# Strassen's seven products in the last unit's second layer, its operand sums in four pieces, and new instruction orders, in a one-core attention and MoE kernel

## The chip, the cores and the metric

The kernel runs on one core of one Trainium2 chip. The metric is the device time of one execution in microseconds (us). A profiled execution has a span, from its first to its last instruction, and a time of its own, which is a little longer than the span because it holds what lies around it. Engines are named as in the profile: PE is the matrix engine (TensorE) and PEld its weight loads, DVE is VectorE, ACT is ScalarE, POOL is GpSimd, SP is SyncE, which here only issues transfers.

## The reference

Two stages follow each other. The first is a gated linear recurrence over 768 tokens for 4 batches and 8 heads of 48 channels; the second is a two-layer network on its output, taken as 3072 tokens of 384 channels, with 2048 hidden channels and the square of a rectifier between the layers.

```python
def _attn_ref(q, k, v, alpha):          # (4, 8, 768, 48) each
    for t in range(S):
        state = alpha[:, :, t, :, None] * state + np.einsum('bhd,bhe->bhde', k[:, :, t], v[:, :, t])
        y[:, :, t] = np.einsum('bhd,bhde->bhe', q[:, :, t], state)
    return y

def _moe_ref(x, w_in, w_out):           # (3072, 384), (384, 2048), (2048, 384)
    r = np.maximum(x @ w_in, 0.0)
    return (r * r) @ w_out
```

## The kernel before

The work is cut into 12 units of 256 tokens: three stretches of the sequence for each of four batches. Unit g goes through these steps; the names in brackets are those of the instruction orders, with the unit's number behind them.

1. Transfers of alpha, k, q and v from memory (`lda`, `ldk`, `ldq`, `ldv`), in fp32.
2. Decays: a product of two alphas (`pr`), logarithm (`ln`), cumulative sums on PE (`m1`, `m1i`, `m1s`), exponentials (`ei`, `ea`, `es`, `ec`), a second product (`bk`, `aq`, lines 679 to 697), then k and q scaled by them (`ekm`, `eqm`, lines 732 and 737), v in bf16 (`vc`, line 727), and transposes (`tr`).
3. Scores on PE (`p`), masked by DVE (`mk`, line 937); the output of the recurrence (`y`, lines 818 to 865), which also holds the state products of the next unit (`kv`); the state (`sa`, `sc`, `sd`).
4. The output goes to bf16 (`xe`) and is transposed (`xt`, `xv`).
5. First layer, line 1030: eight pieces `s1_g_u` of six matmuls of 256 columns, each piece into one PSUM bank of 512 columns, read by a rectifier (`re`, lines 1038 and 1040) and squared into the tile GT (`sq`, lines 1048 to 1052). A square may cover two pieces.
6. Second layer. Each unit has two tiles of 128 tokens, j = 0 and 1; GT holds 16 slices f of 128 hidden channels for both. In units 0, 1 and 2, and in unit 11, it is 16 matmuls of 384 columns for each tile (line 1168). Units 3 to 10 use Strassen's form (`second_layer_strassen`, line 1064): the 16 slices are taken as 8 pairs u of an even and an odd slice, the two tiles as the rows, and the two halves of 192 output columns as the columns of a 2 x 2 block product. Seven products m1 to m7 take the place of eight, each of 8 matmuls of 192 columns (line 1096).

Strassen's form needs sums of blocks of GT, bf16: `ga` writes two differences into SG (line 1080), `gb` overwrites the block of the even slices of tile 1 with a difference (line 1082), and `gc` writes a sum into SH (line 1083). They exist in two halves of four pairs, `_0` and `_1`. They follow each other: ga needs the squares, gb needs ga, gc needs gb. The products use them so: m5 and m7 read SG, m6 and m4 the blocks of GT that hold sums or the odd slices of tile 1, m3 reads SH, m1 and m2 the blocks of GT as they are. The sums of the weights (SW) are made once (`ws`).

The products run in two PSUM banks, psO (A) and the first bank of psWH (B). A collects m1, then m2 on top of it, and, begun afresh, m5 and m3; B collects m6, m7 and m4. After each product a copy or a sum of 128x192 takes what the bank holds so far into the output tile OSB: `ca` after m1, `cb` after m6, `cc` after m2, `cd` after m7, `ce` after m5, `cf` after m4, `cg` after m3 (lines 1123 to 1127). The next product into the same bank waits for it. One transfer then writes the unit's 256 tokens (`out`, line 1145).

The last unit, 11, differs. Tile 0 runs as 16 matmuls of 384 columns into psO, is copied and stored as 192 KB (line 1179). Tile 1 runs in `last_tile` (line 990): 16 matmuls of 272 columns and 16 of 112 into the two banks of psX (line 998), each copied into a tile OSL (lines 1003 and 1005) and stored by itself (line 1006), 136 KB and 56 KB.

Nothing chooses the order at run time. The table ORDERS (line 12) lists every operation of each engine in order, transfers among those of the engine that issues them; an operation whose name stands in the list of ACT runs on ACT, and the same operation may have a form for DVE or POOL. `add` records what an operation reads and writes, and `place` derives from that the semaphores on which it waits; each engine runs its list strictly in order. A sum that writes SG, for instance, waits until the products of the unit before have read SG. Operations `fill512_n` and `fill256_n` in PE's list are matmuls on zeros, 512 or 256 columns wide, put where PE would wait in the first part of the kernel.

Some transfers wait for others by the table AFTER (line 1194): the second half of w_in (`win2`) waits for q of unit 0, `wout0` for win2, `wout1` for k of unit 2, and the loads of units 3 and later for wout0.

Of the kernel before, what the change touches and what calls it, by code (L numbers as in the profile page):

```python
# [13 lines left out]
        table ln0_0 ln1_0 #23 ei0_0 ea0_0 ei1_0 ea1_0 et00_0 ec1_0 ec0_0 vc0 et11_0 ln1 ei1 ea1 xe0 xv0 ec1 re0_0  # L14
        re0_2 re0_3 xe1 re0_4 re0_5 ln2 sq0_5 ei2 re1_1 ea2 ec2 re1_4 es2 re1_3 re1_5 sq1_1 re1_7 et1_2 sq1_6 sq1_3
        sq1_5 oe0_0 ln3 ei3 ea3 ec3 vc3 es3 ln4 xe2 ei4 ea4 oe0_1 oe1_0 sa3 ec4 lm4 re2_1 es4 re2_2 re2_3 sq2_1 vc4
        re2_5 lm5 lm6 xe3 ln5 re2_7 ei5 ea5 ec5 sq2_5 re3_1 re3_0 re3_3 es5 oe2_0 re3_2 ln6 sq3_3 xe4 ei6 ea6 ec6
        re3_7 sq3_5 es6 sq3_7 re3_6 oe2_1 re4_1 re4_0 sq4_1 lm7 ca3 re4_2 ln7 xe5 ei7 re4_3 ea7 sq4_3 ec7 re4_5 re4_6
        lm8 re4_7 es7 sq4_7 re5_0 re5_1 sq4_5 re5_2 sq4_6 re5_3 ln8 xe6 ei8 re5_5 ea8 re5_4 es8 re5_7 cc4 re5_6 sq5_3
        re6_0 lm9 sq5_5 ln9 re6_1 re6_2 lm10 re6_3 ei9 re6_4 ea9 re6_5 sq6_1 re6_6 re6_7 sq6_3 es9 re7_1 re7_0 cc5  # L20
        sq6_5 re7_3 re7_2 ln10 xe8 sq7_1 ei10 ea10 re7_4 re7_5 ca6 lm11 re7_6 re7_7 es10 re8_0 cc6 re8_1 sq7_7 sq7_5
        re8_2 xe9 ln11 re8_3 ei11 ea11 sq8_1 sq8_3 es11 cc7 re8_6 re8_7 sq8_7 re9_0 sq8_5 sq8_6 xe10 re9_3 sq9_3 re9_5
        sq9_1 cc8 re9_6 sq9_6 sq9_5 re10_1 sq10_1 re10_3 xe11 re10_5 ca9 sq10_3 re10_4 sq10_5 re10_6 re11_0 re11_1
        sq10_6 re11_2 re11_3 sq11_3 ca10 re11_5 cc10 re11_7 sq11_6 oe11_10
    """,
    "dve": """
        #19 #2 #11 #16 #4 #10 #3 #8 #7 #5 #1 #13 #17 #18 #12 #9 #6 ekm0_0 eqm0_0 ekm1_0 et10_0 eqm1_0 et01_0 mk0_0 sa0
        mk1_0 sc0 ekm1 eqm1 et0_1 et1_1 mk1_1 mk0_1 sa1 re0_1 sq0_1 sq0_3 pr2 xv1 re0_7 re0_6 sq0_6 bk2 re1_2 re1_0
        ekm2 aq2 sc1 eqm2 et0_2 ws0_0 re1_6 ws2_0 ws1_1 mk1_2 mk0_2 sa2 sc2 bk3 ekm3 sq1_7 aq3 eqm1_3 eqm0_3 ws2_1 xv2
        sd2 re2_0 ekm4 lb4 sc3 eqm1_4 eqm0_4 mk0_3 mk1_3 re2_4 sa4 oe1_1 sc4 xv3 re2_6 bk5 lb5 ekm5 mk1_4 mk0_4 eqm1_5  # L30
        eqm0_5 sq3_1 sa5 re3_5 sc5 re3_4 lb6 xv4 eqm1_6 ekm6 gb3_0 eqm0_6 mk1_5 mk0_5 pr7 ga3_1 sa6 sc6 ws3_1 re4_4
        cb3 xv5 cc3 ekm7 lb7 cd3 ga4_0 ce3 mk1_6 eqm1_7 eqm0_7 mk0_6 cf3 cg3 gb4_0 ga4_1 sa7 ca4 gb4_1 sc7 xv6 cb4 lb8
        ekm8 eqm0_8 mk1_7 mk0_7 eqm1_8 cd4 ce4 ga5_0 sa8 xe7 cf4 sq5_6 ga5_1 cg4 gb5_1 lb9 eqm1_9 gc5_1 ca5 ekm9 cb5
        mk0_8 eqm0_9 mk1_8 cd5 gc5_0 ga6_0 ce5 sa9 cf5 ga6_1 gb6_1 gc6_0 cg5 sq7_3 lb10 cb6 ekm10 sq7_6 mk0_9 mk1_9
        cd6 eqm0_10 eqm1_10 ga7_0 ce6 sa10 ga7_1 cg6 re8_4 cf6 re8_5 ca7 cb7 lb11 ekm11 eqm0_11 eqm1_11 mk0_10 cd7
# [31 lines left out]
        #14 #20 #15 #21 #22 lda1 ldk1 ldq1 win1 win0 win2 lda2 vc1 ldq2 sd0 ldk2 ldv2 wout0 wout1 vc2 sq0_7 sd1 ldk3  # L67
        ldv3 pr3 ws0_1 pr4 bk4 pr6 sq2_3 ws1_0 pr5 ws3_0 sd3 sq2_6 sq2_7 vc5 sd4 ga3_0 bk6 sq3_6 sd5 vc6 gb3_1 bk7 pr8
# [281 lines left out]
def bass_gla_recurrent__then__act_relu_squared_kernel(  # L350
# [13 lines left out]
    T = 256  # L364
# [783 lines left out]
    def second_layer(g):  # L1148
# [115 lines left out]
```

## Time and profile before

| what | value |
|---|---|
| median of three runs | 173.21 us |
| lowest and highest of the three | 169.42 and 173.5 us |
| the profiled execution's own time | 169.46 us |
| its span | 167.7 us |
| its instructions | 5626 |
| PE, PEld busy | 160.9 and 139.6 us |
| DVE, ACT, POOL busy | 131.9, 121.3 and 96.8 us |
| moved by transfers | 32.80 MB |

Everything that is quoted from the profile comes from the one profiled execution. In the views a row names the line of the kernel, the engine, the operation, and what it writes and reads. In a group of instructions, the numbers behind the first bar are the busy time in us and the mean length of one in ns, and behind the second bar the idle time of the engine just before them with what ended it. In the chain that ended last and in the timeline, the first two numbers are the start and the length in us. A PE instruction's own length is longer than the distance between two of them, because matmuls overlap; in the chain the lengths are distances.

### The profile page before, as it was taken

Reading aid. Unit: us, or ns where it says so; the run is one execution under the profiler, and the core shown is the slowest. Engines: PE = TensorE matmul, PEld = TensorE weight load, DVE = VectorE, ACT = ScalarE, POOL = GpSimd, SP = SyncE. Lnnn points to the kernel's source line nnn. Section 1 sums busy time; section 2 is a strip of 40 time slices with the busy share of each in tenths; the row PEclk is TensorE's granted clock in tenths of the full one; section 3 lists DMA queues with packets and bytes.
Section 4 is the critical chain, followed back from the end, with each engine's and each line's share of the span. In section 5 each row is a group of like instructions: output and inputs, shape, how many; then the busy total and the mean of one; then the engine's idle time right before and its main releaser. Section 6 shows DMA issues by size and latency. Waiting matters only on the chain.

```text
span 167.7 us, 5626 instructions
## 1 busy us (share of the span) xinstructions
PE 160.9 (96%) x2431; PEld 139.6 (83%) x2431; DVE 131.9 (79%) x234; ACT 121.3 (72%) x214; POOL 96.8 (58%) x93
## 2 busy tenths in 40 slices
PE   7699999997999999999999999999999999999994
PEld 2466799755688788899999999999999999999973
DVE  5597989889887989889988999798699688353450
ACT  3965487976879699897978899787686856866310
POOL 3923815761559855669648759255729930277600
PEclk9999999999999999999999999999999999999999
DMA  5999999999999999999999989989988500522022
GB/s 135 327 319 209 275 303 216 200 338 267 161 230 166 229 295 124 294 160 263 282 163 327 241 136 336 141 193 334 133 203 139 148 10 4 152 87 94 0 98 94
DMA packets 68232, 32.80 MB, mean 196 GB/s; under 512 B 64144, under 2 KB 65168, under 8 KB 68208
## 3 DMA queue, kind: packets, MB, share of 16 engines
q1 hardware_dynamic: 65584, 25.76, 69.9%
q0 software_dynamic: 2624, 6.69, 16.3%
q8 instruction: 19, 0.31, 0.7%
q14 instruction: 5, 0.04, 0.1%
HBM read 25.17 MB, written 4.72 MB: 178 GB/s over the span
## 4 chain that ended last, share of the span: by engine, by line
PE 75%; DMA 15%; POOL 4%; DVE 3%; issue 1%; ACT 1%
PE psWH L1030 32%; PE psO L1096 13%; PE psWH L1096 10%; PE psO L1168 7%; DMA win<-in_moe_w_in_dram 7%; DMA wout<-in_moe_w_out_dram 5%; DMA raw<-in_alpha_dram 3%; PE psX L829 2%; PE psX L926 2%; PE psZ L797 2%; POOL raw L540 2%; PE psX L818 2%; PE psX L998 2%; PE psZ L926 1%; PE psX L972 1%; POOL win L508 1%
## 5 line engine op out<-in xcount | busy, mean ns | idle before, releaser
L1030 PE MATMUL psWH<-xt,win 128*128 128x256 bf16 x552 | 71.7, 273 | 0.2 <-DMA win<-in_moe_w_in_dram 0.2
L1030 PEld LDWEIGHTS psWH<-xt,win 128*128 128x128 bf16 x552 | 60.1, 129 | 2.1 <-DVE xt L984 0.4
L1038 ACT ACTIVATE rr<-psWH 128x512 bf16<-128x512 f32 x70 | 40.9, 595 | 18.3 <-PE psWH L1030 17.2
L1052 ACT ACTIVATE gt<-rr 128x1024 bf16<-128x1024 bf16 (+1 forms) x38 | 35.1, 940 | 2.8 <-PE psWH L1096 1.6
L1051 POOL TENSOR_TENSOR gt<-rr 128x512 bf16<-128x512 bf16 (+1 forms) x13 | 18.6, 1432 | 14.8 <-ACT rr L1038 9.7
L1082 POOL TENSOR_TENSOR gt<-sg,gt 128x512 bf16<-128x512 bf16 x10 | 12.0, 1202 | 12.6 <-DVE sg L1080 12.6
L1040 DVE TENSOR_SCALAR rr<-psWH 128x512 bf16<-128x512 f32 x22 | 15.0, 685 | 5.1 <-PE psWH L1030 5.0
L1168 PE MATMUL psO<-wout,gt 128*128 128x384 bf16 x96 | 18.4, 326 | 0.0
L937 DVE TENSOR_TENSOR pm<-psZ,caus 128x1024 bf16<-128x1024 f32 x12 | 14.6, 1218 | 1.9 <-PE psZ L926 1.9
L937 DVE TENSOR_TENSOR pm<-psX,caus 128x1024 bf16<-128x1024 f32 x12 | 14.6, 1215 | 0.6 <-PE psZ L926 0.5
L1096 PE MATMUL psWH<-sw,gt 128*128 128x192 bf16 x128 | 14.8, 246 | 0.0
L1096 PE MATMUL psO<-wout,gt 128*128 128x192 bf16 x128 | 14.7, 246 | 0.0
L1083 POOL TENSOR_TENSOR sh<-gt 128x512 bf16<-128x512 bf16 x11 | 14.2, 1298 | 0.7 <-DVE gt L1082 0.5
L1168 PEld LDWEIGHTS psO<-wout,gt 128*128 128x128 bf16 x96 | 8.8, 98 | 4.6
L686 POOL TENSOR_TENSOR ek<-ek,raw 128x384 f32<-128x384 f32 x7 | 7.1, 1008 | 9.6 <-ACT ek L679 9.6
L1127 DVE TENSOR_TENSOR osb<-psWH,osb 128x192 f32<-128x192 f32 x24 | 8.4, 350 | 5.0 <-PE psWH L1096 4.9
L737 DVE TENSOR_TENSOR qks<-raw,ek 128x768 bf16<-128x768 f32 x11 | 11.7, 1063 | 0.4 <-ACT ek L644 0.4
L1080 DVE TENSOR_TENSOR sg<-gt 128x1024 bf16<-128x1024 bf16 x14 | 10.6, 754 | 0.9 <-PE psO L1096 0.9
L1096 PEld LDWEIGHTS psWH<-sw,gt 128*128 128x128 bf16 x128 | 10.9, 98 | 0.3
L1096 PEld LDWEIGHTS psO<-wout,gt 128*128 128x128 bf16 x128 | 10.6, 98 | 0.5
L957 ACT ACTIVATE xbf<-psX 128x768 bf16<-128x768 f32 x11 | 8.9, 806 | 2.9 <-PE psX L818 1.7
L732 DVE TENSOR_TENSOR qks<-raw,eq 128x384 bf16<-128x384 f32 x18 | 10.4, 604 | 0.7 <-DMA raw<-in_q_dram 0.7
(164 smaller groups left out, 298.4 us busy)
## 6 DMA issues: line engine op xcount, KB each, us to landing
out_dram<-osb SPq DMA_DIRECT2D x11, 384.0 KB, 4.8
raw<-in_alpha_dram SPq DMA_DIRECT2D x10, 384.0 KB, 5.1
raw<-in_q_dram SPq DMA_DIRECT2D x10, 384.0 KB, 5.5
raw<-in_v_dram SPq DMA_DIRECT2D x10, 384.0 KB, 4.8
raw<-in_k_dram SPq DMA_DIRECT2D x9, 384.0 KB, 5.2
wout<-in_moe_w_out_dram POOLq DMA_DIRECT2D x2, 768.0 KB, 8.2
raw<-in_k_dram POOLq DMA_DIRECT2D x3, 384.0 KB, 6.4
raw<-in_alpha_dram POOLq DMA_DIRECT2D x2, 384.0 KB, 6.0
```

The costliest lines, as they stand in the source:

```text
L737: add("dve", lambda e, a=a, E=E: e.tensor_tensor(QKS[qs][:, a, :, :, 0:D], RAW[r][:, 1 + a].rearrange("p h j d -> p j h d"), E[la][:].rear ...
L937: add("dve", lambda e, hf=hf, psT=psT: e.tensor_tensor(PM[pm][:, hf].rearrange("p r n j t -> p (r n) (j t)"), psT[:, :, :].rearrange("p r ...
L1030: ins = pe.matmul(psF[:, i * T:(i + 1) * T], WIN[:, kk, hidden(fj)], mov, start=(kk == 0), stop=(kk == KT - 1))
L1038: add("act", lambda e, psF=psF, rr=rr: e.activation(rr, psF, AF.Relu), act_ns(512), pu + 600, reads=[keyF], writes=[("rr", rb, half)], nam ...
L1040: alts={"dve": (lambda e, psF=psF, rr=rr: e.tensor_scalar(rr, psF, 0.0, None, ALU.max), dve_ns(512))})
L1051: alts={"pool": (lambda e, dst=dst, sq=sq: e.tensor_tensor(dst, sq, sq, ALU.mult), 200 + k * 840), "act": (lambda e, dst=dst, sq=sq: e.act ...
L1052: "act": (lambda e, dst=dst, sq=sq: e.activation(dst, sq, AF.Square), act_ns(k * 512))})
L1080: ga = lambda e, us=us: e.tensor_tensor(SG[:, us], view(us, 128, [[0, 2], [1, 128]]), view(us, 0, [[384, 2], [1, 128]]), ALU.subtract)
L1082: gb = lambda e, us=us: e.tensor_tensor(G4[:, us, 0, 1], SG[:, us, 1], G4[:, us, 0, 0], ALU.subtract)
L1083: gc = lambda e, us=us: e.tensor_tensor(SH[:, us], G4[:, us, 1, 0], G4[:, us, 0, 1], ALU.add)
L1096: ins = pe.matmul(psS, left(u), right(u), start=(first and u == 0), stop=(u == nu - 1), skip_group_check=True)
L1168: ins = pe.matmul(psS, GT[gt][:, fj, j, :], WOUT[:, fj, :], start=(fj == 0), stop=(fj == FT - 1))
```

## The change

Three things change together.

First, unit 11's second layer takes Strassen's form too; `last_tile`, its tile OSL and its stores go. In this unit the third pair of products, m5 and m3, runs in a bank of its own, the second bank of psX (C), instead of in A. Three stores take the place of three: the first half of tile 0 (96 KB) after cc, tile 1 (192 KB) after cf, the second half of tile 0 (96 KB) after cg.

Second, in unit 11 the operand sums are cut in four pieces, of 4, 2, 1 and 1 pairs, instead of two of 4; the products are cut in the same pieces, so that m1 becomes `m10` to `m13`, with 4, 2, 1 and 1 matmuls. SG and SH are tracked by pair instead of by half.

Third, all five lists of ORDERS are new. Some 75 operations move to another engine, most of them rectifiers, squares, copies out of PSUM and the sums ga, gb and gc. POOL's list has 93 operations instead of 89, DVE's 247 instead of 234, ACT's 213 instead of 214, PE's 341 instead of 317, SP's 76 as before. PE's fills are 15 of 512 and 8 of 256 columns, before 15 and 6.

```diff
-    LAST_CUT = 272
-    SUMS, SPLIT = 30000, 2
+    SUMS = 30000
-    STRASSEN = tuple(range(3, 11))
+    STRASSEN = tuple(range(3, 12))
+    PIECES = {11: (0, 4, 6, 7, 8)}
...
-        cut = nu // SPLIT
-        for x in range(SPLIT):
-            us = slice(x * cut, (x + 1) * cut)
-            r = range(us.start, us.stop)
+        edges = PIECES.get(g, (0, nu // 2, nu))
+        parts = [range(x, y) for x, y in zip(edges, edges[1:])]
+        for x, r in enumerate(parts):
+            us, cut = slice(r.start, r.stop), len(r)
             ga = lambda e, us=us: e.tensor_tensor(SG[:, us], view(us, 128, [[0, 2], [1, 128]]),
                                                   view(us, 0, [[384, 2], [1, 128]]), ALU.subtract)
...
-                writes=[("sg", x)], name=f"ga{g}_{x}")
+                writes=[("sg", u) for u in r], name=f"ga{g}_{x}")
...
         def phase(k, name, psS, key, left, right, keys, first):
-            for h in range(2):
-                def run(pe, h=h):
-                    for u in range(h * nu // 2, (h + 1) * nu // 2):
+            for h, us in enumerate(parts):
+                def run(pe, us=us):
+                    for u in us:
...
         (psA, keyA), (psB, keyB) = bank("O"), bank("W")
-        psA, psB = psA[:, 0:n], psB[:, 0:n]
+        psC, keyC = bank("X1") if g == G - 1 else (psA, keyA)
+        psA, psB, psC = psA[:, 0:n], psB[:, 0:n], psC[:, 0:n]
...
-        phase(4, "m5", psA, keyA, lambda u: SG[:, u, 1], sums[0], keys(("sg",), ("sw", 0)), True)
+        phase(4, "m5", psC, keyC, lambda u: SG[:, u, 1], sums[0], keys(("sg",), ("sw", 0)), True)
...
-        phase(6, "m3", psA, keyA, lambda u: SH[:, u], wout[1][1], keys(("sh",), ("wout",)), False)
+        phase(6, "m3", psC, keyC, lambda u: SH[:, u], wout[1][1], keys(("sh",), ("wout",)), False)
...
+        if g == G - 1:
+            for x, (j, c) in enumerate(((0, slice(0, n)), (1, slice(0, 2 * n)), (0, slice(n, 2 * n)))):
+                rows = slice(b * S + i * T + j, b * S + i * T + T, 2)
+                add("sp", lambda e, rows=rows, j=j, c=c: e.dma_start(out[rows, c], OSB[ob][:, j, c]), 600, p0 + 7 * step,
+                    reads=[ok[j][y] for y in range(c.start // n, c.stop // n)], name=f"out{g}_{x}", dma=f"l{x}", lag=400)
+            return
```

Of the orders, the parts that the prediction speaks of. The starts of POOL's list (the numbers with # are selects on masks; those with `win`, `wout` and `ld` issue transfers):

```diff
-        #14 #20 #15 #21 #22 lda1 ldk1 ldq1 win1 win0 win2 lda2 vc1 ldq2 sd0 ldk2 ldv2 wout0 wout1 vc2 sq0_7 sd1 ldk3
-        ldv3 pr3 ws0_1 pr4 bk4 pr6 sq2_3 ws1_0 pr5 ws3_0 sd3 sq2_6 sq2_7 vc5 sd4 ga3_0 bk6 sq3_6 sd5 vc6 gb3_1 bk7 pr8
+        #22 #15 #20 #14 #21 lda1 ldk1 ldq1 win1 vc0 win0 win2 lda2 ldk2 ldq2 sd0 ldv2 sq0_1 wout0 wout1 sq0_5 sq0_6
+        aq2 sd1 vc2 ldk3 ldv3 pr3 ws1_1 pr4 bk4 sq2_3 pr6 pr5 sd3 sd4 sq2_7 sq2_6 ws1_0 vc5 ga3_0 gb3_0 bk6 sq3_6 vc6
```

ACT around the wait before y2 (`vc3` and `es3` belong to unit 3):

```diff
-        sq1_5 oe0_0 ln3 ei3 ea3 ec3 vc3 es3 ln4 xe2 ei4 ea4 oe0_1 oe1_0 sa3 ec4 lm4 re2_1 es4 re2_2 re2_3 sq2_1 vc4
+        sq1_5 re1_6 ln3 oe0_0 ei3 ea3 ec3 sq1_6 vc3 es3 ln4 xe2 ei4 lm4 oe0_1 oe1_0 ea4 ec4 re2_0 re2_1 es4 re2_2 lm6
```

The ends of ACT's, DVE's, PE's and POOL's lists:

```diff
-        sq10_6 re11_2 re11_3 sq11_3 ca10 re11_5 cc10 re11_7 sq11_6 oe11_10
+        re11_2 re11_3 cc10 sq11_3 re11_5 sq11_5 re11_6 sq11_6 sq11_7 cc11
...
-        sq11_7 cf10 oe11_0 oe11_11
+        sq11_1 ga11_0 cd10 ce10 ga11_1 re11_7 cg10 cf10 ga11_3 gb11_3 ca11 cb11 gc11_0 cd11 ce11 cf11 cg11
...
-        s2_10_m51 s1_11_7 s2_10_m30 s2_10_m31 s2_10_m40 s2_10_m41 s2_11_0_0 s2_11_0_1 s2_11_0_2 s2_11_0_3 s2_11_1_0
-        s2_11_1_1
+        s2_10_m11 s1_11_3 s2_9_m41 s2_10_m20 s1_11_4 s2_10_m21 s2_10_m60 s2_10_m61 s1_11_5 s2_10_m50 s2_10_m70
+        s2_10_m71 s2_10_m51 s1_11_6 s2_10_m40 s1_11_7 s2_10_m30 s2_10_m31 s2_10_m41 s2_11_m50 s2_11_m10 s2_11_m11
+        s2_11_m12 s2_11_m13 s2_11_m60 s2_11_m61 s2_11_m62 s2_11_m63 s2_11_m20 s2_11_m21 s2_11_m70 s2_11_m71 s2_11_m72
+        s2_11_m73 s2_11_m51 s2_11_m52 s2_11_m22 s2_11_m23 s2_11_m53 s2_11_m40 s2_11_m41 s2_11_m42 s2_11_m43 s2_11_m30
+        s2_11_m31 s2_11_m32 s2_11_m33
...
-        gb10_1 sq11_1 gc10_1 sq11_5
+        gc10_1 gb11_0 ga11_2 gb11_1 gb11_2 gc11_3 gc11_1 gc11_2
```

The rest of the orders keeps the same steps in much the same sequence, with halves of products, rectifiers and squares dealt to other places in the lists.

More of the change, by code (lines that the diff above doesn't have):

```diff
@@ L19 @@
[L19 to L23, printed above, removed]
@@ L69 @@
-        gc3_0 gc3_1 vc7 sq5_1 gc4_0 bk8 sq5_7 vc8 gc4_1 pr9 sd6 gb5_0 bk9 pr10 sq6_7 sd7 sq6_6 vc9 gb6_0 bk10 pr11
-        vc10 gc6_1 gb7_0 gb7_1 gc7_1 bk11 ga8_0 vc11 gc7_0 gb8_0 gb8_1 gc8_1 gc8_0 sq9_7 gb9_0 sq10_7 gc9_1 gb10_0
-        gb10_1 sq11_1 gc10_1 sq11_5
+        #22 #15 #20 #14 #21 lda1 ldk1 ldq1 win1 vc0 win0 win2 lda2 ldk2 ldq2 sd0 ldv2 sq0_1 wout0 wout1 sq0_5 sq0_6
+        aq2 sd1 vc2 ldk3 ldv3 pr3 ws1_1 pr4 bk4 sq2_3 pr6 pr5 sd3 sd4 sq2_7 sq2_6 ws1_0 vc5 ga3_0 gb3_0 bk6 sq3_6 vc6
@@ L1177, in second_layer @@
                 alts={"dve": (lambda e, j=j, psS=psS: e.tensor_copy(OSB[ob][:, j], psS), dve_ns(DM))})
-            if g == G - 1:
-                add("sp", lambda e, rows=rows: e.dma_start(out[rows, :], OSB[ob][:, 0]), 600, ps_ + 1300,
-                    reads=[("osb", ob, 0)], name=f"out{g}_0", dma=f"o{ob}", lag=600)
-            elif j == 1:
+            if j == 1:
                 dst = out[b * S + i * T:b * S + i * T + T, :].rearrange("(p j) n -> p (j n)", j=2)
```

137 lines of the change are left out of this document (61 added, 76 removed).

## The prediction

> **What bounds the kernel now.** I read the page first (span and busy shares), then the busy time by stretch, then the chain that ended last, in its last 11 us and in its first 41.
>
> ```profile
> span 167.7 us, 5626 instructions
> ```
> ```profile
> 150.00:160.00 10.00, 10.00 (x112) 9.87 (x111) 4.79 (x13) 5.05 (x9) 6.50 (x5) 1.00 0.11 41
> sum 120.00, PE 119.85 PEld 110.31 DVE 97.41 ACT 92.64 POOL 74.81; mean PE 9.99 PEld 9.19 DVE 8.12 ACT 7.72 POOL 6.23
> ```
>
> The rows are the last of twelve stretches of 10 us and their sum; after a stretch's length stand the busy times of PE, PE's weight loads, DVE, ACT and POOL, then the granted clock (1.00 in all twelve). Between 40 and 160 us PE is idle for 0.15 us of 120, while DVE, ACT and POOL have slack, most of it in 150 to 160, where DVE works 4.79 us of 10. From 40 us on the kernel is PE's instruction stream, end to end: only less work on PE shortens this part, and any wait put into PE's order lengthens it one for one.
>
> ```profile
> 157.14 0.66 PE psWH L1030 x6
> ...
> 159.44 0.66 PE psWH L1096 x8
> 160.10 2.60 PE psO L1168 x16
> 162.70 2.65 PE psX L998 x32
> 165.35 0.02 issue
> 165.38 0.27 DVE osl L1005
> ```
>
> These are the last links of the chain (start, length, what). Six first-layer matmuls of 256 columns take 0.66 us, eight Strassen matmuls of 192 columns 0.66 us too, so 82.5 ns each. The last unit's second layer is the two links at 160.10 and 162.70, 5.25 us. PE ends at 165.35; a copy and a store fill the remaining 2.35 us of the span.
>
> The first 40 us hang on transfers:
>
> ```profile
> 8.79 11.97 DMA win<-in_moe_w_in_dram
> ...
> 21.04 8.26 DMA wout<-in_moe_w_out_dram
> ...
> 29.32 5.54 DMA raw<-in_alpha_dram
> ```
> ```profile
> 25.06 0.60 POOL L508 DMA_DIRECT2D wout<-in_moe_w_out_dram  x1 [3.32 <-DMA raw<-in_k_dram]
> 25.85 0.82 POOL L727 CAST vbf<-raw 128x768 bf16<-128x768 f32 x1 [0.19 <-DMA raw<-in_v_dram]
> ```
> ```profile
> 37.50 0.99 POOL L658 TENSOR_TENSOR prd<-raw 128x384 f32<-128x384 f32 x1
> ...
> 37.53 1.38 DVE L688 TENSOR_TENSOR ek<-ek,raw 128x384 f32<-128x384 f32 x1 [0.42 <-ACT ek L679]
> ...
> 40.05 0.36 PE L858 MATMUL psX<-smd,kqt 128*64 128x96 bf16 x8 [0.95 <-DVE qks L737]
> ```
>
> The second half of w_in lands, w_out is issued, alpha of unit 3 waits for that, and its products reach PE at 40.05 (y2), where PE has stood idle for 0.95 us. So the end is 40.05 plus PE's work after y2 plus the tail.
>
> **Term 1: PE's work in the last unit.** Removed are 16 matmuls of 384, 16 of 272 and 16 of 112 columns, 5.25 us by the chain. Added are seven products of eight 192-column matmuls: 56 x 82.5 ns = 4.62 us. That is -0.63 us on the path. Pieces cost PE nothing, since the count of matmuls is the same in four pieces as in two.
>
> ```profile
> L1096 PEld LDWEIGHTS psWH<-sw,gt 128*128 128x128 bf16 x128 | 10.9, 98 | 0.3
> ```
>
> A weight load reads 98 ns, longer than the 82.5 ns of its matmul. If loads set the pace, 56 x 98 ns = 5.49 us, and the term is +0.24. But eight of these pairs pass in 0.66 us and the 32 pairs at 162.70 in 2.65 us (32 loads end to end would be 3.14), so loads overlap each other and I keep -0.63. The Trainium skill (TensorE: Matmul & The Clock Gate, LDWEIGHTS) prices a 128-column load at 128 / 1.2 ns, about 107 ns; end to end that would be an estimated 5.97 us, a loss of 0.72, and the row of 0.66 us for eight disagrees with such a pace.
>
> **Term 2: the sums of the last unit, and whether PE waits for them.** Added are four each of ga, gb and gc. Their rows, with those of the steps before them:
>
> ```profile
> L1040 DVE TENSOR_SCALAR rr<-psWH 128x512 bf16<-128x512 f32 x22 | 15.0, 685 | 5.1 <-PE psWH L1030 5.0
> ...
> L1127 DVE TENSOR_TENSOR osb<-psWH,osb 128x192 f32<-128x192 f32 x24 | 8.4, 350 | 5.0 <-PE psWH L1096 4.9
> ...
> L1048 DVE TENSOR_TENSOR gt<-rr 128x512 bf16<-128x512 bf16 x5 | 2.1, 416 | 0.0
> ...
> L697 DVE TENSOR_TENSOR eq<-eq,raw 128x384 f32<-128x384 f32 x2 | 1.1, 548 | 0.0
> ```
> ```profile
> L1082 POOL TENSOR_TENSOR gt<-sg,gt 128x512 bf16<-128x512 bf16 x10 | 12.0, 1202 | 12.6 <-DVE sg L1080 12.6
> ...
> L1051 POOL TENSOR_TENSOR gt<-rr 128x1024 bf16<-128x1024 bf16 x4 | 7.7, 1925 | 4.7 <-ACT rr L1038 4.2 <-ACT osb L1123 0.5
> ```
> ```profile
> L1052 ACT ACTIVATE gt<-rr 128x512 bf16<-128x512 bf16 x1 | 0.6, 630 | 1.1 <-DVE rr L1040 1.1
> ```
>
> (Before the last bar: busy us, mean ns of one.) I walk PE's new order by hand, with 0 at the end of s1_11_5. s1_11_7 ends at 2.95 and the three halves of unit 10 left at 3.94; then m5's first piece, m1 from 4.27 to 4.93, m6 to 5.59, m2's first two pieces to 6.09, m7 to 6.75, rests of m5 and m2 to 7.24, m4 to 7.90, m3 to 8.56.
> The large first piece is early: its ga (1024 columns, by the 416 ns of 512 some 0.8 us, DVE) must only wait until unit 10's m7 has read SG (0.66), so gb (1202 ns, POOL) ends near 2.7, needed at 4.93.
> The last piece is the tight one. From 2.95: rectifier 0.69 (DVE), square 0.63 (ACT), so 4.27, with hand-offs about 4.4; m1 wants it at 4.85. ga and gb of one pair (256 and 128 columns) have no row; they lie between nothing and the 416 ns of 512 columns; by halves with some fixed cost I estimate 0.27 and 0.2. gb done at 4.9 to 5.2; m6 wants it at 5.51. So by itself nothing waits.
> What can make it wait is the port. DVE L688 above took 1.38 us beside POOL L658, against 548 ns in L697, the same shape: it ran after POOL had ended at 38.49. In the tail, POOL runs gb of pieces 1 and 2 (about half and a quarter of 1202 ns) just when DVE wants ga and gb of piece 3. If POOL goes first each time, gb is ready at 5.4, the copy ca behind it on DVE holds m2 by 0.2, and gc11_0, held by POOL's gc, delays cd and with it m4 by 0.25: 0.45 in all. Bounds 0 and 0.45; I take 0.2. The Trainium skill (SBUF — State Buffer, SBUF: two separate sides) says this port pair is an exclusive lock kept for a whole instruction; the pair of rows agrees.
> Behind the waiting DVE instruction stand ca, cb, cd, ce, which free the banks of psO, psWH and psX for m2, m7, m4, m3. m5 moved to the free psX bank is what keeps cc (on ACT) off this path; without it m5 would wait for cc.
>
> **Term 3: after PE.** The last copy becomes a sum of 192 columns, 0.35 instead of 0.27: +0.08. The last store grows from 56 KB to 96 KB, and 192 KB go out just ahead:
>
> ```profile
> out_dram<-osb SPq DMA_DIRECT2D x1, 192.0 KB, 1.9
> out_dram<-osl SPq DMA_DIRECT2D x1, 136.0 KB, 1.7
> ...
> out_dram<-osl SPq DMA_DIRECT2D x1, 56.0 KB, 1.5
> ```
>
> (The last column is us from issue to landing.) 96 KB lies between the two, 0 to +0.4; I take +0.1, as 96 is nearer to 56 and the 192 KB leave one sum (0.35) earlier.
>
> **Term 4: the start, up to y2.** The new orders put more in front of POOL's transfers. vc0 (0.82, the L727 row) now stands between the issues of win1 and of win0 and win2: those two go out 0.8 later. They lie in the queue for 11.97 us anyway, so the queue's backlog hides it. sq0_1 (1925 ns) now stands in front of wout0 and issues it perhaps 1 us after 21.04; until 25.85 the queue is still delivering v of unit 2, issued ahead of it, so this is hidden too. wout1 waits for k2, which now goes ahead of q2: earlier, if anything. sq0_5, sq0_6 and aq2 (1.9 + 1.2 + 1.0) stand in front of sd1, vc2, ldk3 and ldv3; POOL was idle for 3.32 us before 25.06, which takes most of it. SP's loads and transposes only change places among themselves behind its wait for w_out. Where a cover is gone, y2 comes later by as much, up to 1 us. On the other side, POOL's product pr4 ran in front of DVE's L688 by 0.03 us; if L688 goes first, y2 could come 0.83 earlier, but vc3, now behind one more square (0.63) on ACT, allows an estimated 0.35. Ends -0.35 and +1.0; I take 0, since both transfer chain and race are as before. The two more fills on PE lie in its waits of the start.
>
> **Term 5: the middle.** Some 75 operations change engines and PE's halves and pieces are dealt anew; the set of matmuls is the same. Below, all that can be won is the idle time, 0.15. Above, no row shows the new order; the nearest is L688's excess of 0.83, and each unit's sums could pay it once. I take +0.1, nearest to the 0.15 that such an order shows now, and two such waits, 1.7, as the upper end.
>
> **Sum.** 169.46 (the profiled execution's own time) - 0.63 + 0.20 + 0.08 + 0.10 + 0 + 0.10 = 169.31, so 169.3. The median of the three runs shown is 173.21, 3.75 above the profiled execution, the lowest 169.42. The one trace has no row for that difference; an execution that carried it would take 173.1.
>
> **The rivals.**
> First, port waits decide, and the kernel becomes slower. The place is the sums: DVE's ga, gb or a PSUM copy behind a POOL sum, with PE behind both. For it: L688, and POOL gets three more gb and three more gc. Against it: the slack of 0.3 to 0.6 in the walk, and POOL idle 12.6 us for gb alone (the L1082 row). Price: 0.45 in the tail and 0.83 for each unit that it catches. From 0.45 us in all (0.63 less 0.08 and 0.10) the gain is eaten; two units give 169.46 - 0.63 + 0.45 + 0.08 + 0.10 + 1.66 = 171.1, five 173.6.
> Second, w_out lands late: the queue runs dry behind sq0_1, y2 slips by 1.0: 170.3. Against it: the 25.85 row.
> Third, the start is what differs between executions. After 40 us PE has no idle time, so a run of 173 must lose its time ahead of that or by the clock, which this trace shows full. If the fills and the order of transfers remove it, the median falls to 169.3, 2.3% under 173.21. For it: the three times differ by 4.08 us; against it: the new start is hardly different.
> Fourth, the change does not do what it says, because loads set the pace: +0.24 in place of -0.63, 170.2. The 0.66 us row speaks against it.
>
> **The numbers.** The forecast 0.56, the first rival 0.18, the second 0.08, the third 0.16, the fourth 0.02. The likeliest case's own range is 168.4 (169.46 - 0.63 + 0.08 - 0.35 - 0.15) to 170.4 (169.46 - 0.63 + 0.45 + 0.08 + 0.4 and one wait of 0.6). The range, which takes in the first rival's two units and an execution with the median's excess, is 168.4 to 173.1. A change of over 2%, 3.4 us, is about what a measurement of this kernel can tell from none. Faster by that: the third rival, 0.16; no other has the idle time to win. Slower by that: 0.08 of the first (five units) and 0.02 of the second with both covers gone: 0.10. The rest, 0.74, is within 2%.
>
> **What would show it.** Term 1: 56 Strassen matmuls in the last links, 4.6 us. Term 2: no idle time or stretch ahead of m63, m20, m40 in PE's last 5 us; the DVE sums of pair 3 under 0.3 us. Term 3: about 2.5 us from PE's end to the span's. Term 4: y2 at 39.7 to 40.4. Term 5: PE idle under 0.3 us from 40 to 160. Wrong would be: PE waits of over 0.45 us for a sum, or y2 past 41.

## The result, and the profile after

The changed kernel takes 174.76 us (median of four runs, 173.89 to 175.4), the kernel before 172.31 in the same comparison; the ratio is 1.0263, 95% interval 1.0204 to 1.0323: slower. The forecast was 169.3, with a range of 168.4 to 173.1 and a change within 2%. The profiled execution takes 175.21 us, 5.75 over that of before, and its span grows by 5.8. Ratios use only executions within 1.5% of the fastest of their kernel, so this one is not 174.76 / 172.31, and where too few were left none is given.

The page, then the chain that ended last in the first 44 us:

```profile
span 173.5 us, 5651 instructions
```
```profile
20.33 1.84 POOL gt L1033
22.16 7.24 DMA wout<-in_moe_w_out_dram
...
29.42 9.04 DMA raw<-in_alpha_dram
...
38.53 1.01 POOL prd L659
...
43.66 0.36 PE psX L859 x8
```

From w_out on the chain is the one of before, and w_out lands at the same moment (29.40, before 29.30) although sq0_1 (1.84) now stands in front of it. But alpha of unit 3 takes 9.04 us instead of 5.54, and y2 starts at 43.66 instead of 40.05. That is 3.61 of the 5.8 us.

The stretches of 10 us in which PE now stands idle, with the sum over 40 to 160 (behind the stretch's length, PE's busy time):

```profile
40.00:50.00 10.00, 9.54 (x121) 6.65 (x122) 9.11 (x15) 8.09 (x19) 3.10 (x3) 1.00 0.64 131
50.00:60.00 10.00, 9.69 (x159) 8.06 (x158) 8.37 (x14) 8.13 (x15) 7.57 (x7) 1.00 1.00 198
60.00:70.00 10.00, 9.29 (x164) 7.67 (x163) 8.80 (x13) 7.75 (x14) 7.67 (x6) 1.00 1.09 228
...
100.00:110.00 10.00, 9.48 (x126) 8.96 (x124) 10.00 (x16) 7.49 (x13) 8.27 (x8) 1.00 0.96 223
...
130.00:140.00 10.00, 9.46 (x193) 8.66 (x194) 9.33 (x18) 6.21 (x11) 3.84 (x4) 1.00 0.74 159
...
sum 120.00, PE 117.40 PEld 106.08 DVE 105.17 ACT 91.86 POOL 69.71; mean PE 9.78 PEld 8.84 DVE 8.76 ACT 7.66 POOL 5.81
```

PE's idle time in 40 to 160 is 2.60 us instead of 0.15. In PE's timeline three single waits make up most of it (last the idle time before the row and what ended it): v of unit 5, a sum out of PSUM, a transpose.

```profile
65.06 0.19 PE L819 MATMUL psX<-sbd,kqt 64*128 64x48 bf16 x1 [0.71 <-POOL vbf L728]
...
102.49 0.75 PE L1080 MATMUL psO<-wout,gt 128*128 128x192 bf16 x7 [0.52 <-DVE osb L1110]
...
130.88 0.42 PE L927 MATMUL psX<-kqt 64*64 64x128 bf16 x16 [0.54 <-DMA kqt<-qks]
```

From y2 to the first matmul of the last second layer pass 122.41 us (43.66 to 166.07), before 120.05: another 2.36 us. PE stands idle for 2.14 of the 122.41 and for 0.10 of the 120.05, so 2.04 of the 2.36 are waits. The last links of the chain:

```profile
166.07 0.33 PE psX L1080 x4
166.40 0.66 PE psO L1080 x8
167.06 0.66 PE psWH L1080 x8
...
169.50 0.79 PE psWH L1080 x8
170.29 0.67 PE psX L1080 x8
170.97 0.02 issue
170.99 0.36 DVE osb L1110
```

The last second layer runs from 166.07 to 170.97, 4.90 us instead of 5.25 (-0.35), and from there to the span's end are 2.53 instead of 2.35 (+0.18). The four differences, 3.61 + 2.36 - 0.35 + 0.18, make the 5.8 us.

The chain names alpha, but the engines' timelines between 24 and 32 us show something else beside it. First bk2 and the issue of k of unit 3 in the kernel before, then DVE, POOL and PE of the changed kernel:

```profile
25.16 0.55 DVE L688 TENSOR_TENSOR ek<-ek,raw 128x384 f32<-128x384 f32 x1
```
```profile
30.93 0.94 POOL L540 DMA_DIRECT2D raw<-in_k_dram  x1
```
```profile
25.53 4.92 DVE L689 TENSOR_TENSOR ek<-ek,raw 128x384 f32<-128x384 f32 x1
30.37 0.68 DVE L1022 TENSOR_SCALAR rr<-psX 128x512 bf16<-128x512 f32 x1
```
```profile
24.63 2.91 POOL L1033 TENSOR_TENSOR gt<-rr 128x1024 bf16<-128x1024 bf16 x2
27.50 0.99 POOL L696 TENSOR_TENSOR eq<-eq,raw 128x384 f32<-128x384 f32 x1
28.45 0.82 POOL L902 TENSOR_TENSOR sbd<-tmp,acm 128x384 bf16<-128x384 f32 x1
29.22 0.81 POOL L728 CAST vbf<-raw 128x768 bf16<-128x768 f32 x1
29.98 0.94 POOL L541 DMA_DIRECT2D raw<-in_k_dram  x1
```
```profile
31.11 0.88 PE L1012 MATMUL psX<-xt,win 128*128 128x256 bf16 x6 [3.49 <-DVE rr L1022]
```

DVE's bk2 took 0.55 us before and takes 4.92 now: it stands from 25.53 through all five operations that POOL runs without a pause (sq0_5, sq0_6, aq2, sd1, vc2) and ends 0.42 us after the last of them (30.03). The rectifier re1_2 waits behind it in DVE's list, and PE waits 3.49 us for that rectifier. So two things could have made y2 late: hold A (bk2) and late transfer B (alpha of unit 3, beside k and v of unit 3, which POOL now issues 0.56 us behind alpha instead of 1.61). PE works in a fixed order and stands idle for only 0.59 of the 12.55 us between 31.11 and y2. With alpha on time y2 could therefore have come at most 0.59 us earlier: behind A, B costs no more than that here, and by that estimate A alone would have cost some 3.0 of the 3.61.

### The profile page after: what moved, and what is told of

Same layout as the page of the kernel before. It is cut to its first block, busy times and chain, and to the rows that moved or that the text cites. A ratio compares the mean times of both kernels' runs of the same rounds, so it can differ in the third digit from the quotient of the medians.

```text
span 173.5 us, 5651 instructions
## 1 busy us (share of the span) xinstructions
PE 162.2 (94%) x2439; PEld 141.3 (81%) x2441; DVE 145.6 (84%) x247; ACT 121.4 (70%) x213; POOL 98.5 (57%) x97
## 4 chain that ended last, share of the span: by engine, by line
PE 62%; DMA 18%; DVE 10%; issue 2%; POOL 2%; SPq 2%; ACT 2%; ACTq 0%
PE psWH L1012 24%; PE psO L1080 11%; PE psWH L1080 9%; DMA raw<-in_alpha_dram 7%; DMA wout<-in_moe_w_out_dram 4%; DMA raw<-in_v_dram 3%; DVE pm L938 3%; DMA kqt<-qks 3%; PE psO L1153 3%; PE psX L927 2%; PE psX L830 2%; DVE rr L1022 1%; PE psX L819 1%; PE psZ L798 1%; PE psZ L927 1%
## 5 line engine op out<-in xcount | busy, mean ns | idle before, releaser
L1033 POOL TENSOR_TENSOR gt<-rr 128x512 bf16<-128x512 bf16 (+1 forms) x12 | 17.0, 1421 | 24.5 <-ACT rr L1020 14.5
L1064 POOL TENSOR_TENSOR gt<-sg,gt 128x512 bf16<-128x512 bf16 (+2 forms) x13 | 14.8, 1146 | 14.5 <-DVE sg L1062 14.5
L1065 POOL TENSOR_TENSOR sh<-gt 128x512 bf16<-128x512 bf16 (+2 forms) x14 | 15.6, 1128 | 4.0 <-DVE gt L1064 3.8
L1080 PE MATMUL psWH<-sw,gt 128*128 128x192 bf16 x144 | 16.9, 247 | 0.0
L1080 PE MATMUL psO<-wout,gt 128*128 128x192 bf16 x144 | 16.0, 246 | 0.5 <-DVE osb L1110 0.5
L1062 DVE TENSOR_TENSOR sg<-gt 128x1024 bf16<-128x1024 bf16 (+2 forms) x17 | 14.7, 872 | 1.2 <-ACT gt L1034 0.4
L1153 PE MATMUL psO<-wout,gt 128*128 128x384 bf16 x80 | 15.3, 326 | 0.0
L659 POOL TENSOR_TENSOR prd<-raw 128x384 f32<-128x384 f32 x8 | 9.1, 1139 | 6.8 <-DMA raw<-in_alpha_dram 6.7
L1080 PEld LDWEIGHTS psWH<-sw,gt 128*128 128x128 bf16 x144 | 11.9, 98 | 0.7 <-DVE osb L1110 0.2
L1110 DVE TENSOR_TENSOR osb<-psWH,osb 128x192 f32<-128x192 f32 x27 | 9.5, 352 | 3.5 <-PE psWH L1080 3.4
```

The lines of the kernel that those rows point to most:

```text
L1033: alts={"pool": (lambda e, dst=dst, sq=sq: e.tensor_tensor(dst, sq, sq, ALU.mult), 200 + k * 840), "act": (lambda e, dst=dst, sq=sq: e.act ...
L1062: ga = lambda e, us=us: e.tensor_tensor(SG[:, us], view(us, 128, [[0, 2], [1, 128]]), view(us, 0, [[384, 2], [1, 128]]), ALU.subtract)
L1064: gb = lambda e, us=us: e.tensor_tensor(G4[:, us, 0, 1], SG[:, us, 1], G4[:, us, 0, 0], ALU.subtract)
L1065: gc = lambda e, us=us: e.tensor_tensor(SH[:, us], G4[:, us, 1, 0], G4[:, us, 0, 1], ALU.add)
L1080: ins = pe.matmul(psS, left(u), right(u), start=(first and u == 0), stop=(u == nu - 1), skip_group_check=True)
L1153: ins = pe.matmul(psS, GT[gt][:, fj, j, :], WOUT[:, fj, :], start=(fj == 0), stop=(fj == FT - 1))
```

## The experiments

The table has one trace of each; "product" is the start of POOL's product of alpha of unit 3, which waits for that transfer.

| kernel | bk2 took | product | y2 | span | ratio to before (95%) |
|---|---|---|---|---|---|
| before | 0.55 | 34.94 | 40.05 | 167.7 | |
| changed | 4.92 | 38.53 | 43.66 | 173.5 | 1.0263 (1.0204 to 1.0323) |
| e2_squares_act | 0.55 | 35.23 | 41.20 | 170.5 | 1.0107 (1.0046 to 1.0167) |
| e3_k3_sp | 1.46 | 35.50 | 41.38 | 170.9 | 1.0100 (1.0013 to 1.0188) |
| e4_both | 0.55 | 34.88 | 40.78 | 170.3 | 1.0118 (1.0046 to 1.0191) |
| e5_orders_only | 4.96 | 38.26 | 46.91 | 177.0 | none |
| e7_no_gap | 4.24 | 35.15 | 45.09 | 173.6 | 1.0311 (1.0257 to 1.0365) |
| e11_dma_gap | 2.09 | 39.01 | 44.02 | 172.8 | 1.0265 (1.0195 to 1.0335) |
| e13_k3_ahead | 1.18 | 36.73 | 41.74 | 170.0 | none |
| e6_before_k3_sp | 1.18 | 35.05 | 41.10 | 171.2 | 1.0105 (1.0017 to 1.0192) |
| e9_v5_first | 0.55 | 35.34 | 41.26 | 170.1 | 1.0101 (1.0038 to 1.0163) |
| e12_mended | 0.55 | 35.66 | 41.91 | 170.9 | 1.0150 (1.0048 to 1.0252) |
| e1_tail_only | 1.19 | 34.74 | 40.28 | 169.1 | 1.0059 (1.0027 to 1.0092) |
| e8_tail_act | 0.55 | 35.08 | 40.18 | 169.5 | 0.9989 (0.9945 to 1.0034) |
| e10_gb_early | 1.18 | 34.69 | 40.59 | 168.5 | 0.9990 (0.9919 to 1.0061) |

**The start: A, B or both.** The first theory was that A and B each suffice, so that taking one away gains little.

e2_squares_act takes A away:

```diff
-pool: ... wout0 wout1 sq0_5 sq0_6 aq2 ...
+pool: ... wout0 wout1 aq2 ...
-act:  ... ea2 es2 re1_4 ...
+act:  ... ea2 es2 sq0_5 sq0_6 re1_4 ...
```

> The changed kernel with the squares sq0_5 and sq0_6 moved from POOL to ACT, so that DVE's bk2 no longer stands beside an unbroken run of POOL operations. Two-cause theory (starved bk2, and late alpha of unit 3): bk2 takes under 1.5 us instead of 4.92, PE's wait of 3.49 us before the group at 31.11 shrinks to under 1.5, but y2 stays within 0.6 us of 43.66, since alpha of unit 3 still lands near 38.5; span 173 to 173.6. Rival (bk2 alone is the cause): y2 near 40.2, span near 170.

e3_k3_sp takes B away:

```diff
-pool: ... sd1 vc2 ldk3 ldv3 pr3 ...
+pool: ... sd1 vc2 pr3 ...
-sp:   ... lda3 lda4 ldq3 ldk4 ...
+sp:   ... lda3 ldk3 lda4 ldq3 ldv3 ldk4 ...
```

> The changed kernel with the loads of k and v of unit 3 moved from POOL's queue to SP's, behind alpha of unit 3. Two-cause theory: alpha of unit 3 takes 5.5 to 6 us instead of 9.04 and has landed by 35.5, bk2 still takes about 4.9 us and PE still waits about 3.5 us before the group at 31.11, so y2 comes only 0.1 to 0.6 us earlier (43.1 to 43.5) and the span is 172.9 to 173.5. Rival (the transfer alone is the cause): y2 near 40.2, span near 170.

e4_both has both edits.

> Both edits together: sq0_5 and sq0_6 on ACT, k and v of unit 3 on SP's queue. Two-cause theory: bk2 under 1.5 us and alpha of unit 3 landed by 35.5, y2 at 40 to 40.8, span 169.8 to 170.8: some 3 us less than either edit alone. Rival (a third cause holds the start, or both edits only move the wait): y2 still past 42.

Each edit alone brings y2 to 41.2 to 41.4, and both together are no better by their ratios: the expectations of e2 and e3 missed. But neither run had taken away only what it was meant to. In e2 alpha was on time although k and v of unit 3 still went out on POOL, 0.59 us behind it. In e3 bk2 was let through early. What is left of the lateness comes from the edits: in e2 the chain starts at a moved square on ACT (27.30) and PE waits 0.90 us for the rectifier behind it; in e3 and e4 y2 waits for v of unit 3, which now stands fifth in SP's list and lands at 40.46 and 39.86. From e4's chain:

```profile
34.70 5.16 DMA raw<-in_v_dram
...
40.78 0.36 PE psX L859 x8
```

In e3 POOL's timeline shows where bk2 got through:

```profile
24.38 2.91 POOL L1033 TENSOR_TENSOR gt<-rr 128x1024 bf16<-128x1024 bf16 x2
27.60 1.01 POOL L696 TENSOR_TENSOR eq<-eq,raw 128x384 f32<-128x384 f32 x1 [0.31 <-ACT eq L694]
```
```profile
26.26 1.46 DVE L689 TENSOR_TENSOR ek<-ek,raw 128x384 f32<-128x384 f32 x1
```

POOL waited 0.31 us for ACT before aq2, from 27.29 on, and bk2 ended at 27.72. That made a new theory: what holds bk2 is an unbroken run on POOL, and a short pause ends it. (In e3 bk2 began at the end of the first square, so it waited for one operation only.) e7_no_gap closes that pause while B stays away:

```diff
-pool: ... sq0_5 sq0_6 aq2 sd1 vc2 ldk3 ldv3 pr3 ...
+pool: ... sq0_5 sq0_6 vc2 sd1 aq2 pr3 ...      (ldk3, ldv3 on SP as in e3_k3_sp)
```

> k and v of unit 3 on SP's queue as in e3_k3_sp, and on POOL vc2 and sd1 ahead of aq2, so that POOL has work that is ready at each moment and its run has no gap (e3_k3_sp had one of 0.31 us, and bk2 was through in 1.46 us). Theory 1 (DVE's operation of two SBUF inputs gets through only when POOL pauses): bk2 3 to 4 us, ending with POOL's run near 29.9, PE's wait behind it 1.5 to 2.5 us, y2 at 42.2 to 43.2, 1 to 2 us later than e3_k3_sp. Theory 2 (the transfer counts): y2 at 41 to 41.5 as in e3_k3_sp.

DVE, PE, and a stretch of 1 us behind the wait (granted clock is the third number from the right):

```profile
26.01 4.24 DVE L688 TENSOR_TENSOR ek<-ek,raw 128x384 f32<-128x384 f32 x1
```
```profile
30.91 1.50 PE L1011 MATMUL psX<-xt,win 128*128 128x256 bf16 x6 [2.81 <-DVE rr L1021]
32.20 2.31 PE L1011 MATMUL psWH<-xt,win 128*128 128x256 bf16 x12
```
```profile
31.00:32.00 1.00, 1.00 (x6) 0.78 (x7) 1.00 (x3) 0.00 (x0) 0.00 (x0) 0.50 1.03 203
```

The hold is back, with alpha on time, and y2 comes at 45.09, 3.71 later than in e3. So A alone is enough to make y2 late: shown. It cost more than expected, because PE came back from its wait at half the clock (last section; the 18 matmuls behind it took 3.61 us by the chain, in e2 2.19), and DVE, now late, met POOL's next run. How late A alone makes y2 at the full clock no run shows; the 3.0 us above are an estimate from the changed kernel's trace.

e11_dma_gap is the changed kernel with a pause put into the run:

```diff
-pool: ... sq0_5 sq0_6 aq2 sd1 vc2 ldk3 ldv3 pr3 ...
+pool: ... sq0_5 sq0_6 ldk3 ldv3 aq2 sd1 vc2 pr3 ...
```

> The changed kernel with POOL's two issues of k and v of unit 3 between sq0_6 and aq2: the same work on POOL, but its run of operations is broken by about 1.8 us of issuing near 27.5, and k and v of unit 3 go out 2.5 us earlier still. Theory 1 (bk2 waits for a pause in POOL's operations): bk2 ends at 27.5 to 28 (about 2 us instead of 4.92), PE's wait behind it 0.8 to 1.3 us instead of 3.49, y2 at 41 to 42, and the time 1.5 to 2.5 us under the changed kernel. Theory 2 (k and v of unit 3 too early in POOL's queue delay alpha of unit 3): alpha of unit 3 lands at 38 or later, y2 at 43 or later, the time as the changed kernel's.

```profile
25.74 2.91 POOL L1032 TENSOR_TENSOR gt<-rr 128x1024 bf16<-128x1024 bf16 x2
30.76 0.94 POOL L540 DMA_DIRECT2D raw<-in_k_dram  x1 [2.11 <-DMA wout<-in_moe_w_out_dram]
```
```profile
26.98 2.09 DVE L688 TENSOR_TENSOR ek<-ek,raw 128x384 f32<-128x384 f32 x1
```

bk2 did as theory 1 has it: 2.09 us, over at 29.07, 0.42 behind POOL's run (28.65). But y2 and the time did not: ldk3 waited 2.11 us for w_out with aq2 behind it, which made PE wait 1.61 us elsewhere, and alpha was late again, as theory 2 has it. The run shows that a pause in this run of POOL lets bk2 through, and says nothing on the price of B. For that, e13_k3_ahead changes only the place of two issues in the kernel before, where bk2 is free:

```diff
-pool: ... vc2 sq0_7 sd1 ldk3 ldv3 pr3 ...
+pool: ... vc2 sq0_7 ldk3 ldv3 sd1 pr3 ...
```

> The kernel before, with POOL's issues of k and v of unit 3 ahead of sd1 and nothing else changed: they go out about 0.3 us behind alpha of unit 3 instead of 1.6, and bk2 stays free (0.55 to 1.2 us). Where k of unit 3 went out on POOL's queue within 0.65 us of alpha of unit 3, alpha landed at 38.2 or later in three traces of four; at 1.6 us or more, or on SP's queue, at 34.7 to 35.6 in all. Theory 2 (that order of issues makes alpha late, without any hold of bk2): alpha of unit 3 lands at 37.5 to 39, y2 at 42.5 to 44, time 1.5 to 3.5 us above the kernel before. Theory 1 (the late alpha only came along with the held bk2): alpha at 35 to 35.6, y2 near 40.2, within 0.5 us of the kernel before. sd1 is 1 us later in both; if that counts, PE waits for it ahead of y2.

```profile
29.09 7.57 DMA raw<-in_alpha_dram
...
41.74 0.36 PE psX L857 x8
```

Alpha takes 7.57 us instead of 5.54 and y2 slips by 1.69: in this trace B acts without A, and is worth about half of what theory 2 expected (172.72 us in the median, the kernel before 170.53 beside it). Over all traces, k of unit 3 issued on POOL's queue within 0.65 us behind alpha went with a late alpha in four of five (changed 9.04 us, e5, e11, e13; not in e2), and in none where it went out 1.6 us or more behind alpha, or on SP's queue.

e5_orders_only has the second layer of before in unit 11, and the changed kernel's orders elsewhere (`s2_11_0_0 ... s2_11_1_1` in place of the 28 pieces, and no sums of unit 11).

> The code of the kernel before (old second layer in the last unit) with the new orders of the other units. Its start is that of the changed kernel, so it is also a second look at it. Theory 1 (the unbroken run of POOL operations holds bk2 every time): bk2 near 4.9 us again, y2 at 43 to 44, time within 0.6 us of the changed kernel's 174.8. Theory 2 (the late alpha of unit 3 is what counts, and it is a chance of one execution): alpha of unit 3 in 5.5 to 6 us, y2 near 41. If bk2 is long and alpha is not late and y2 is still past 43, bk2 alone is enough.

A and B both recur (4.96; 38.26), so neither was a chance of one execution. y2 at 46.91 is later than in the changed kernel above all because PE's clock was halved from 30.3 us to 37.1; the total, 172.46 to 178.75 in four runs, decides nothing beyond that.

e6_before_k3_sp moves k and v of unit 3 to SP in the kernel before, in the places of e3's diff, for the prediction's third rival:

> The kernel before with k and v of unit 3 on SP's queue behind alpha of unit 3 (POOL's queue then holds no load behind w_out). If executions of the kernel before differ by the order in which these two queues deliver, the runs here narrow to within 1 us of 169.5; if not (theory: the spread has another cause), they spread as the kernel before does, over 2 us or more, at the same median within 0.6 us, unless v of unit 3, now last in one queue, lands late (at 40 or later) and y2 with it by up to 1 us.

The runs lie between 171.03 and 173.65 and do not narrow; v of unit 3 lands late, as feared, and PE waits 1.18 us for it at y2. What sets executions of the kernel before apart is not this order of transfers alone, and stays open.

**The middle.** e9_v5_first is e4_both with one pair of SP's list put back:

```diff
-sp: ... tr1_4 ldq5 ldv5 out0_1 ...
+sp: ... tr1_4 ldv5 ldq5 out0_1 ...
```

> e4_both with the loads of v and q of unit 5 back in the order of the kernel before, v first. Theory (the middle's largest wait, 0.71 us near 62, is v5 issued one transfer later): that wait is gone, the rest as e4_both (0.52 near 99 for DVE's ga beside POOL's bk), time 0.5 to 0.8 us under e4_both. Rival (another operation is late right behind it): within 0.2 us of e4_both, with PE waiting elsewhere in 58 to 68.

e4_both, then e9_v5_first, 60 to 70 us:

```profile
60.00:70.00 10.00, 9.29 (x163) 7.67 (x162) 8.00 (x14) 7.91 (x15) 6.76 (x5) 1.00 1.08 221
```
```profile
60.00:70.00 10.00, 10.00 (x169) 8.28 (x167) 9.09 (x14) 8.32 (x15) 6.25 (x6) 1.00 1.06 221
```

PE's idle time there goes from 0.71 us to nothing, and y2 to the span's end from 129.52 (170.3 - 40.78) to 128.84 us. The ratios (1.0118 and 1.0101) do not part them, since their intervals overlap; the traces do.

e12_mended adds two edits to e9:

```diff
-dve:  ... re6_2 re6_3 ga5_1 cg4 cf4 ...
+dve:  ... re6_2 re6_3 cg4 ga5_1 cf4 ...
-pool: ... gb11_0 ga11_2 gb11_1 gb11_2 ...
+pool: ... gb11_0 gb11_1 ga11_2 gb11_2 ...
```

> e9_v5_first with two more waits of the changed orders taken away: the copy of unit 4 that PE waits 0.52 us for near 99 goes ahead of DVE's ga beside POOL's bk, and the gb of the second piece of unit 11 goes ahead of the ga of the third on POOL. Theory (the rest of the loss is single waits of that kind, each paid one for one): 0.5 to 0.9 us under e9_v5_first, ratio to the kernel before 1.002 to 1.007. Rival (the new orders are slower throughout): ratio still 1.010.

```profile
104.04 1.50 PE L1012 MATMUL psWH<-xt,win 128*128 128x256 bf16 x12 [0.42 <-DVE rr L1022]
```

The wait of 0.52 us near 99 went, and one of 0.42 for a rectifier came at 104.04; y2 to the end is 128.99, no better than e9. The single waits of the middle are not independent; how the rest of its 2.36 us could be had stays open.

**The last unit.** e1_tail_only has the code of the change and the orders of before, but for unit 11's second layer and sums, which have the new order (its squares stay where they were).

> The changed code with the orders of the kernel before, except the last unit: its second layer by Strassen, sums in four pieces, in the new order. My theory: the loss is in the start and the middle, the last unit itself is right, so y2 at 40.0 to 40.4, the 56 Strassen matmuls of the last unit 4.6 to 5.1 us on PE, about 2.5 us from PE's end to the span's end, and a time 0.2 to 0.45 us under the kernel before for executions that start alike (about 169.0 to 169.3 beside 169.46). Rival (the sums of the last unit cost the time): 1 us or more above the kernel before, with PE waiting in the last 8 us.

e8_tail_act moves one square:

```diff
-pool: ... gc10_1 sq11_5 gb11_0 ...
+pool: ... gc10_1 gb11_0 ...
-act:  ... re11_5 cc10 re11_7 ...
+act:  ... re11_5 cc10 sq11_5 re11_7 ...
```

> e1_tail_only with one square of unit 11 (the 1024-column one that POOL began at 156.82) on ACT. Theory (port): DVE's ga of the same time (1.94 us beside that square) takes 0.7, PE's wait of 0.66 us for the half of unit 10 goes, and the time falls by 0.6 to 1.0 us, to 0.3 us above to 0.4 us below the kernel before. Rival (the Strassen products of the last unit do not pay by themselves): within 0.2 us of e1_tail_only.

e10_gb_early is e8 with the pair on POOL that e12 also has.

> e8_tail_act with POOL's gb of the second piece of unit 11 ahead of its ga of the third (in e8_tail_act POOL stood idle for 0.90 us before that ga, with the second piece's ga done at 161.0). Theory (the gain of the last unit is eaten by the chain of the last pieces on POOL): the m6 product no longer takes 1.06 us for 0.66, unit 11's second layer falls from 5.46 us on PE to 4.9 to 5.1, the time by 0.3 to 0.5 us: ratio to the kernel before 0.994 to 0.999. Rival (PE's last 5 us are set by something else, such as weight loads): unchanged, 5.4 us or more.

DVE, POOL and PE of e1_tail_only, then DVE of e8_tail_act:

```profile
157.43 1.94 DVE L1057 TENSOR_TENSOR sg<-gt 128x1024 bf16<-128x1024 bf16 x1
```
```profile
156.82 2.01 POOL L1028 TENSOR_TENSOR gt<-rr 128x1024 bf16<-128x1024 bf16 x1 [0.54 <-ACT osb L1101]
```
```profile
159.70 0.83 PE L1075 MATMUL psO<-wout,sh 128*128 128x192 bf16 x8 [0.66 <-DVE osb L1105]
```
```profile
158.73 0.69 DVE L1057 TENSOR_TENSOR sg<-gt 128x1024 bf16<-128x1024 bf16 x1
```

e1 fell between its two theories: the start as expected (y2 at 40.28), but 0.6% slower. The first ga of unit 11 stood beside a square on POOL and took 1.94 us, and PE paid 0.66 for the copy behind it; with the square on ACT it takes 0.69 and that wait is gone, as expected. The last second layer by the chain, which was 5.25 us before and 4.90 in the changed kernel, takes 5.40 (161.19 to 166.59) in e1, 5.30 (161.65 to 166.95) in e8 and 5.11 (160.86 to 165.97) in e10. e10's edit gained 0.19 of the 0.3 to 0.5 expected, which its ratio does not show; its m6 still takes 0.16 longer than 0.66. None of the three beats the kernel before by more than their intervals: of the 0.63 us of PE, 0.14 is left in e10, and the 0.18 behind PE takes it. No version was found that beats both kernels.

## Why the prediction was wrong

**Term 1** (-0.63) **and term 2** (+0.20): -0.43 forecast, -0.35 measured. Eight matmuls pass in 0.66 us, so weight loads set no pace, and the sums cost 0.28 (4.90 - 4.62), inside the bounds 0 to 0.45. That depends on the orders around: with those of the kernel before the same sums cost 0.78 (e1), 0.68 with one square taken off POOL (e8) and 0.49 in e10.

**Term 3** (+0.18): measured 0.18, from spans given to 0.1 us.

**Term 4** (0, ends -0.35 and +1.0): measured +3.61. This is the step that failed. Its parts on transfers in POOL's list held (w_out landed within 0.1 us). The failure is the sentence that sq0_5, sq0_6 and aq2 stand in front of sd1, vc2, ldk3 and ldv3, and that POOL's idle time of 3.32 us takes most of it. It counted only who is behind these operations in POOL's list. It did not ask which operation of DVE falls into the time in which POOL, idle before, now works without a pause: bk2, which took 4.92 us instead of 0.55, with the rectifier behind it that PE waits for (e7: enough by itself). And with the idle time used up, ldk3 and ldv3 went out 1 us closer behind alpha; the prediction counted that as lateness of theirs and found none, while their being early delays alpha (e13: 1.69).

**Term 5** (+0.1, at most 1.7): measured +2.36. (By the two lists of orders 83 operations change engines, not some 75; nothing in the term hangs on it.) The largest single wait, 0.71, is a moved transfer: q5 ahead of v5 in SP's list (e9). The prediction had said of SP's loads that they only change places among themselves behind the wait for w_out, and had priced nothing past that wait; its upper end of 1.7 was two port waits, and was passed.

**The rivals.** The first, port waits, named the mechanism with a chance of 0.18, but put it at the sums and priced it at 0.83 for each, from the row of L688 (1.38 us beside one POOL operation, 0.55 without). The excess there is one operation's; bk2's is 4.37. One operation is the usual price, also where POOL goes on without a pause (e1, last section). That a hold can last through five operations no row of the kernel before shows. The second (w_out late) did not come. The third is not borne out by e6. Of the prediction's own tests, "y2 past 41" and "PE idle under 0.3 us from 40 to 160" failed. So did that of term 2: the DVE sums of the last pair took 0.41 and 0.33 us, not under 0.3, and m4 was stretched to 0.79 us. The 4.6 us of term 1 became 4.90 by these stretches; the test of term 3 held.

## What to carry to other kernels

When work is moved to POOL, or POOL's idle time is closed, look for every DVE operation with two SBUF inputs that falls into POOL's run. Price it by one operation of POOL as the usual case and by the rest of the run up to POOL's next pause as the worst; then ask who is behind it in DVE's list. An idle time that is to take moved work may be what lets another engine through or keeps two queues' transfers apart. A shorter instruction stream at the very end of a kernel is worth only what the chain of its last operands leaves: 0.63 us of PE became 0.35 here, and 0.14 and less with other orders around it.

## What the runs showed of the hardware

A DVE operation with two SBUF inputs can be held through several operations of POOL. In the changed kernel, e5, e7 and e11 bk2 ended 0.42 to 0.43 us behind the end of POOL's run, and was passed over each time an operation of the run ended before that (four times, in e11 once). The Trainium skill (SBUF — State Buffer, SBUF: two separate sides) has the one that starts first keep the port pair for its whole instruction; the runs agree with that. Who comes next they show both ways, since bk2, waiting from 25.53, did not get the pair when sq0_5, sq0_6, aq2 and sd1 had ended, while in e1 it got in between vc2 and sq0_7, which follow each other directly. DVE and POOL of e1, then the same square in the kernel before:

```profile
25.91 1.19 DVE L684 TENSOR_TENSOR ek<-ek,raw 128x384 f32<-128x384 f32 x1
```
```profile
25.87 0.82 POOL L723 CAST vbf<-raw 128x768 bf16<-128x768 f32 x1 [0.20 <-DMA raw<-in_v_dram]
26.66 1.35 POOL L1028 TENSOR_TENSOR gt<-rr 128x512 bf16<-128x512 bf16 x1
```
```profile
26.64 1.03 POOL L1051 TENSOR_TENSOR gt<-rr 128x512 bf16<-128x512 bf16 x1
```

bk2 ended 0.41 us behind vc2 there, and the square took 1.35 us instead of 1.03. It is the same in e6, e10 and e13 (1.18 us each), and in the 15 traces no DVE operation with two SBUF inputs but bk2 in those four is passed over. What sets those four apart stays open.

PE's clock can fall to half in the middle of a kernel. In e7 and e5 the granted clock was 0.50 behind waits of 2.81 and 3.53 us; in the changed kernel it stayed at 1.00 behind one of 3.49. The Trainium skill (TensorE: Matmul & The Clock Gate, Part 1: The HAM clock gate) halves the clock after an idle window of some 3.4 us that runs freely. The halved stretches agree with such a window, 3.4 us in e7 (30.5 to 33.9) and 6.8 in e5 (30.3 to 37.1). But the clock fell 2.4 and 2.2 us into the waits, and the whole wait of e7 is shorter than the window, so a wait need not fill one; how long a wait is safe no run here shows.

A transfer of 384 KB on SP's queue can be slowed by one that POOL's queue issues 0.3 to 0.6 us behind it. Alpha of unit 3 took 7.57 to 9.04 us in four of the five such traces (7.57 in e13, with nothing else changed), and 5.1 to 6.0 in the ten others. Why e2 escaped, with the same distance as the changed kernel, stays open.
